# Key chunks of a values tile 400 bytes apart instead of 388, in an attention kernel on one core

## Chip, cores, metric

The kernel runs on one core of one Trainium2 chip. The metric is device time in microseconds (us) of one run; the timed runs of one kernel beside each other lay within about 0.1% here. PE is TensorE (matmul), PEld its weight loads, DVE is VectorE, ACT is ScalarE.

## The reference, cut to what matters

The input `x` (2048 x 640) is normalised; a gated feed-forward branch makes a gate from it, and an attention branch with 32 heads of width 192 makes the value that is gated. Only the last 512 rows of the key and value caches are used.

```python
q = (xn @ wq)                                   # 32 heads x 192
scores = einsum("bhqd,bhkd->bhqk", q, k) * (192 ** -0.5)
p = softmax(scores, axis=-1)                    # over 512 keys
o = einsum("bhqk,bhkd->bhqd", p, v)             # <- the matmuls of this study
s = o.reshape(...) @ wo
return x + s * silu(glu_branch(xn))
```

## The kernel before

The 512 keys are 4 chunks of 128 (`KC = 4`), `DH = 192`. Each of four values tiles holds, in every partition, 4 chunks of 192 values of bf16 (384 bytes) with a column of ones behind each, which makes the softmax denominator come out of the same matmul as a 193rd column, and one column of padding: 194 columns, 388 bytes from chunk to chunk.

```python
    NV = 2 * G                                             # 4 tiles
    v_tiles = []
    for i in range(NV):
        vt = v_pool.tile([P, KC, DH + 2], BF16, name=f"v_sb{i}")
        nc.vector.memset(vt[:, :, DH:DH + 1], 1.0)
        v_tiles.append(vt)
    # ... cut ...
    def load_v(hp, eng):
        # ... cut: tile (2 * hp + i) % NV for head i of pair hp ...
            eng.dma_start(
                vt[:, :, 0:DH],
                A_v_cache[0, hk, Sk - W:Sk, :].rearrange("(p j) d -> p j d", j=KC),
            )
    # ... cut ...
    def stage_pv(n, pp, i):
        # ... cut ...
        E, vt = E_t[n, pp], v_t[hp][i]
        o_ps = bank2()[:, :, 0:2 * OW].rearrange("p b (i n) -> p b i n", i=2)
        for q in range(TQ):                                # 4 blocks of 128 queries
            for c in range(KC):                            # 4 key chunks
                nc.tensor.matmul(                          # L429
                    o_ps[:, q // 2, q % 2, 0:DH + 1], lhsT=E[:, c, i, q * P:(q + 1) * P],
                    rhs=vt[:, c, 0:DH + 1],
                    start=(c == 0), stop=(c == KC - 1),
                )
        # ... cut: reciprocal of column DH, multiply, transpose by DMA ...
```

So a values chunk is the moving operand of a 128x193 matmul, 2048 of them in the program, in groups of 16, and successive matmuls walk the chunks 0, 1, 2, 3, 0, 1, ... of one tile. L397 makes q, L413 the scores, L429 is the value matmul, L474 the output projection.

The softmax here doesn't subtract the row's maximum and nothing guards it: scores larger than these inputs give would overflow.

Of the kernel before, what the change touches and what calls it, by code (L numbers as in the profile page):

```python
# [10 lines left out]
BF16 = mybir.dt.bfloat16  # L11
# [4 lines left out]
def kernel(  # L16
# [14 lines left out]
    P = 128  # L31
# [5 lines left out]
    _, Hkv, Sk, DH = A_k_cache.shape  # L37
# [7 lines left out]
    KC = W // P  # L45
# [50 lines left out]
    v_pool = ctx.enter_context(tc.tile_pool(name="v_pool", bufs=1, **rs))  # L96
# [8 lines left out]
    NV = 2 * G  # L105
    v_tiles = []
    for i in range(NV):
        vt = v_pool.tile([P, KC, DH + 2], BF16, name=f"v_sb{i}")
        nc.vector.memset(vt[:, :, DH:DH + 1], 1.0)
        v_tiles.append(vt)  # L110

# [488 lines left out]
```

## Time and profile before

| | before |
|---|---|
| time, median of the first 3 runs | 932.78 us (932.74 to 933.32) |
| span in the profile | 931.2 us |
| PE busy | 918.3 us, 99% |
| value matmuls (L429): busy, mean duration | 193.7 us, 247 ns |
| PE waiting for others, in all | 3.5 us |

The page of the kernel before, the summary by engine and, in 40 slices of the span, the PE row and the clock row (a 9 is 90% or more):

```profile
PE 918.3 (99%) x7946; PEld 549.5 (59%) x8025; DVE 450.7 (48%) x639; ACT 302.2 (32%) x340; POOL 129.5 (14%) x170
...
PE   9999999999999999999999999999999999999997
...
PEclk9999999999999999999999999999999999999999
```

The waits of PE (engine, tile, line that waited, who was waited for: us in total, times, longest):

```profile
PE ps_all L249 <- DVE warm L244: 1.3, 1, 1.3
PE ps_all L413 <- DVE o_st L436: 1.1, 3, 0.6
PE ps_all L261 <- ACT xnT L276: 0.8, 2, 0.5
PE ps_all L397 <- DVE o_st L436: 0.3, 1, 0.3
```

PE is busy for 99% of the span and waits for almost nothing (3.5 us), at a granted clock of 1.000. But matmuls overlap in this record: each of them lasts 247 ns and the next starts 82 to 87 ns after it, long before it ends. The groups of instructions (busy us, mean ns | idle before), the value line's own view (duration minimum/median/maximum), and the timeline of the first stretch in which value matmuls run alone (start us, length us, group, count):

```profile
L429 PE MATMUL ps_all<-v_sb,E 128*128 128x193 bf16 x2048 | 193.7, 247 | 0.1
```

```profile
L429 PE MATMUL ps_all<-v_sb,E x2048: 243/247/258, 200.8 to 914.5; 128*128 128x193 bf16 x187
```

```profile
200.82 11.05 PE L429 MATMUL ps_all<-v_sb,E 128*128 128x193 bf16 x128
212.47 0.82 PE L413 MATMUL ps_all<-qT,kT 64*128 64x512 bf16 x6 [0.59 <-DVE o_st L436]
```

The last fence: 128 matmuls back to back in 11.05 us. The finest reading is the interval from one matmul's start stamp to the next one's. No view of the profile prints it; it is worked out from the start stamps in the trace and averaged by chunk within the groups of 16 (the first and last matmul of each group left out of the averages by chunk). For the kernel before it is 82.5, 86.3, 85.7, 85.9 ns after chunks 0, 1, 2, 3. (Without the second matmul of each group, whose interval is 87.4 ns, chunk 1 has 86.0 ns, the figure of the prediction.) The sum over four matmuls is taken as a third of the time from the second to the fourteenth start of a group: 340.5 ns, the same in all four tiles.

### The profile page before, as it was taken

The numbers are of one execution on the slowest core, as the hardware profiler recorded it, in microseconds if no ns is written. First come the engines' busy times: TensorE is split into PE (matmuls) and PEld (weight loads), VectorE is DVE, ScalarE is ACT, GpSimd is POOL, SyncE is SP. The second block draws the span as 40 slices with busy tenths as digits, with TensorE's granted clock in tenths as the row PEclk, the third lists the DMA queues.
The fourth block names the chain that finished last, engine by engine and source line by source line (L and its number), as shares of the span: only waits on it lengthen the run. The fifth ranks groups of instructions, "written<-read, shape, count | busy, mean of one in ns | idle before, by whom it ended". The sixth has DMA issues, their size and how long they took to land. (4 is left out here: it accounts for less than half of the span.)

```text
span 931.2 us, 18098 instructions
## 1 busy us (share of the span) xinstructions
PE 918.3 (99%) x7946; PEld 549.5 (59%) x8025; DVE 450.7 (48%) x639; ACT 302.2 (32%) x340; POOL 129.5 (14%) x170
## 2 busy tenths in 40 slices
PE   9999999999999999999999999999999999999997
PEld 5545445465756565656565656566665656566665
DVE  5443532443535454545454444444454545454477
ACT  4333322345141414242423233232323242424320
POOL 0021100010002000200020002000200010395800
PEclk9999999999999999999999999999999999999999
DMA  9544430145425343533453344434342434373755
GB/s 292 146 91 102 67 98 16 57 66 86 80 53 112 77 77 61 111 77 71 67 107 81 57 80 87 102 51 86 77 111 52 86 77 111 75 175 78 148 147 148
DMA packets 176959, 87.17 MB, mean 94 GB/s; under 512 B 152240, under 2 KB 171312, under 8 KB 176880
## 3 DMA queue, kind: packets, MB, share of 16 engines
q1 hardware_dynamic: 146864, 47.20, 26.0%
q0 software_dynamic: 6656, 22.81, 10.1%
q10 hardware_dynamic: 23360, 15.99, 6.2%
q8 instruction: 63, 1.03, 0.5%
q14 instruction: 16, 0.13, 0.1%
HBM read 44.70 MB, written 5.24 MB: 54 GB/s over the span
## 5 line engine op out<-in xcount | busy, mean ns | idle before, releaser
L417 ACT ACTIVATE E<-ps_all 128x1024 bf16<-128x1024 f32 x256 | 246.1, 1023 | 490.4 <-PE ps_all L413 374.2
L402 DVE CAST qT<-ps_all 128x1024 bf16<-128x1024 f32 x96 | 117.5, 1225 | 235.9 <-PE ps_all L397 233.4
L474 PE MATMUL ps_all<-wo_g,oT 128*128 128x128 bf16 (+2 forms) x1474 | 224.3, 295 | 3.2
L397 PE MATMUL ps_all<-xnT,wqp 64*128 64x512 bf16 x960 | 222.2, 376 | 0.3 <-DVE o_st L436 0.3
L397 PE MATMUL ps_all<-xnS,wqp 64*128 64x512 bf16 x960 | 221.4, 376 | 0.0
L429 PE MATMUL ps_all<-v_sb,E 128*128 128x193 bf16 x2048 | 193.7, 247 | 0.1
L413 PE MATMUL ps_all<-qT,kT 64*128 64x512 bf16 x1536 | 184.1, 376 | 1.1 <-DVE o_st L436 1.1
L429 PEld LDWEIGHTS <-E 128*128 128x128 bf16 x2048 | 171.6, 98 | 19.3 <-issue 7.2
L474 PEld LDWEIGHTS <-oT 128*128 128x128 bf16 x1536 | 121.3, 97 | 76.6
L397 PEld LDWEIGHTS <-wqp 64*128 64x128 bf16 x1920 | 100.4, 100 | 107.7 <-issue 0.8
L413 PEld LDWEIGHTS <-kT 64*128 64x128 bf16 x1536 | 74.6, 94 | 91.4 <-issue 6.1
L436 DVE TENSOR_TENSOR o_st<-ps_all,rden 128x768 bf16<-128x768 f32 x128 | 122.6, 957 | 8.1 <-DMA oT<-o_st 3.4
L507 DVE TENSOR_TENSOR acc<-ps_all,acc 128x640 f32<-128x640 f32 x96 | 79.2, 825 | 42.7 <-PE ps_all L474 42.7
L435 DVE RECIPROCAL rden<-ps_all 128x4 f32<-128x4 f32 x128 | 23.3, 182 | 84.4 <-PE ps_all L429 84.2
L131 POOL COPY k_sb<-kn_sb 128x768 bf16<-128x768 bf16 x32 | 25.9, 832 | 274.3 <-DMA kT<-k_sb 227.3
L326 DVE TENSOR_TENSOR hT_sb<-ps_all,sig_sb 128x512 bf16<-128x512 f32 x48 | 33.1, 692 | 51.0 <-PE ps_all L320 41.2
L152 POOL DMA_DIRECT2D wqp<-in_A_wq_dram x16 | 11.8, 741 | 320.9 <-PE ps_all L397 271.8
L320 PE MATMUL ps_all<-xnT,wu_sb 128*128 128x512 bf16 x220 | 55.6, 379 | 0.3
L320 PE MATMUL ps_all<-xnT,wg_sb 128*128 128x512 bf16 x220 | 55.5, 379 | 0.3
L340 PE MATMUL ps_all<-wd_sb,hT_sb 128*128 128x128 bf16 (+1 forms) x377 | 52.4, 298 | 0.4
L325 ACT ACTIVATE sig_sb<-ps_all 128x512 bf16<-128x512 f32 x48 | 28.6, 597 | 56.6 <-PE ps_all L320 56.2
L340 PEld LDWEIGHTS <-hT_sb 128*128 128x128 bf16 x384 | 29.7, 98 | 23.1
(49 smaller groups left out, 271.3 us busy)
## 6 DMA issues: line engine op xcount, KB each, us to landing
wqp<-in_A_wq_dram POOLq DMA_DIRECT2D x16, 480.0 KB, 6.6
wo_g<-in_A_wo_dram ACTq DMA_DIRECT2D x8, 960.0 KB, 5.9
kn_sb<-in_A_k_cache_dram POOLq DMA_DIRECT2D x32, 192.0 KB, 4.5
v_sb<-in_A_v_cache_dram ACTq DMA_DIRECT2D x28, 192.0 KB, 2.9
gB_d<-gB_sb POOLq DMA_DIRECT2D x16, 160.0 KB, 2.2
xnS<-xnT SPq DMA_DIRECT2D x8, 320.0 KB, 4.9
gBa_sb<-gB_d POOLq DMA_DIRECT2D x16, 160.0 KB, 2.9
xa_sb<-in_A_x_dram POOLq DMA_DIRECT2D x16, 160.0 KB, 3.2
```

The source lines that it names most:

```text
L320: nc.tensor.matmul(gu[:, i, :], lhsT=w[:, c, f * P:(f + 1) * P], rhs=xnT[s][:, c, :], start=(c == 0), stop=(c == NCD - 1),)
L325: nc.scalar.activation(sig_sb[:], gu[:, 0, :], AF.Sigmoid)
L326: nc.vector.tensor_tensor(hT_sb[:, f, :], gu[:, 1, :], sig_sb[:], ALU.mult)
L340: nc.tensor.matmul(oB_ps[:, d0:d0 + dsz], lhsT=hT_sb[:, f, q * P:(q + 1) * P], rhs=wd_sb[:, f, d0:d0 + dsz], start=(f == 0), stop=(f == NF ...
L397: nc.tensor.matmul(ps[:, b, :], lhsT=wq_t[g][r, 2 * c + h, u::PC], rhs=x[s][r, c, :], start=(c == 0 and h == 0), stop=(c == NCD - 1 and h ...
L402: nc.vector.tensor_copy(qT_t[n][:, u, :, :], ps)
L413: nc.tensor.matmul(ps[:, b, :], lhsT=kT[r, c * PC + j, :], rhs=qT[r, j, pp, :], start=(j == 0), stop=(j == PC - 1),)
L417: nc.scalar.activation(E_t[n, pp][:, c, :, :], ps, AF.Exp, scale=scale_qk)
L429: nc.tensor.matmul(o_ps[:, q // 2, q % 2, 0:DH + 1], lhsT=E[:, c, i, q * P:(q + 1) * P], rhs=vt[:, c, 0:DH + 1], start=(c == 0), stop=(c = ...
L436: nc.vector.tensor_tensor(o_st[:, :, i * DH:(i + 1) * DH].rearrange("p (b i) d -> p b i d", b=2), o_ps[:, :, :, 0:DH], rden[:].to_broadcas ...
L474: nc.tensor.matmul(oA[:, d0 - base:d0 - base + dsz], lhsT=oT_t[n, pp][:, q * PC + j, :], rhs=wo_t[g][:, cc, d0:d0 + dsz], start=(cc == 0), ...
L507: nc.vector.tensor_tensor(acc[t][:], oA[:, 0:D], acc[t][:], ALU.add)
```

## The change

The intent: make every chunk start on a 16-byte boundary (400 = 25 x 16; 388 is 24 x 16 + 4). The tile bases are multiples of 32 bytes in both built programs. Instructions and their order stay the same on every engine.

```diff
-        vt = v_pool.tile([P, KC, DH + 2], BF16, name=f"v_sb{i}")
+        vt = v_pool.tile([P, KC, DH + 8], BF16, name=f"v_sb{i}")
```

## The prediction

> **What bounds the kernel now.** TensorE. The busy summary gives PE 918.3 us of a 931.2 us span (99%), DVE 48%, ACT 32%; the clock is 9 tenths or more throughout. The waits view charges the matmuls only 3.5 us of waiting. Busy time of pipelined matmuls can flatter, so I read start-to-start times in the trace: each shape keeps its own pitch almost without gaps (512 columns 215-216 ns, 128 columns 55-56 ns). What shortens a matmul's pitch should shorten the span one for one.
>
> **What the change touches.** The 2048 value matmuls (128x193 bf16; values tile moving, E stationary), about 174 us of starts. Every group of 16 walks 4 queries x 4 key chunks. Chunk c starts at base + 388c bytes before, base + 400c after. In the built programs all four bases are multiples of 32 bytes, so before only chunk 0 is 16-byte aligned; chunks 1-3 sit 4, 8 and 12 bytes past such a boundary. No instruction is added or removed, and the order on every engine stays.
>
> The trace separates the chunks. From a chunk's start to the next matmul's:
> - chunk 0: 82.5 ns (duration 244)
> - chunks 1, 2, 3: 86.0, 85.6, 85.9 ns (duration 247)
>
> The view of this line shows the same as minimum 243 and median 247. [...]the others are about 3.3 ns above. Chunk 0 is also the first of each sum, but the 128-column output-projection matmuls keep 55-56 ns whether first or not. [...]3.3 ns is about 8 columns, 16 bytes of bf16, so an estimate: a misaligned start costs one more line. Counting lines doesn't give it: 386 bytes touch 25 lines at offsets 0, 4, 8 and 12 alike.
>
> **Cost.** Removed: (3.5 + 3.1 + 3.4) ns x 512 = 5.1 us, all on PE, all critical. Added: nothing on engines. Moved: each values tile grows by 48 bytes a partition; the value loads still write 384-byte pieces, land in about 3 us, and PE doesn't wait for them. Weight loads take 98 ns but overlap: chunk 0 already runs at 82.5 ns with the same kind of load. DVE and ACT have slack for a 4% faster value stage.
>
> **Predicted time: 927.8 us**, 8 in 10 between 926.7 and 930.0. Chances: faster by over 2% 0.01, within 2% 0.98, slower by over 2% 0.01.
>
> **What would show each step right.** Value matmuls: all four chunks near 82.5 ns start to start, mean duration about 244 instead of 247, busy about 188 us instead of 193.7; other pitches, clock and PE's waits unchanged; span about 5 us shorter.
>
> **What would make it wrong.** (1) The boundary that matters is 32 bytes, not 16: chunks 1 and 3 then sit 16 bytes past one, only chunk 2 gains, about 1.6 us (931.2 us). The trace of before has no moving operand at such an address. (2) Chunk 0 is fast for its place in the sum in this loop alone: no gain. (3) Weight loads back up once all four run at 82.5 ns: part of the gain. (4) The faster value stage makes PE wait for a PSUM bank that DVE empties or for E: the waits view would grow by what is lost.

"The others" are chunks 1 to 3, with 85.8 ns on average about 3.3 ns above chunk 0's 82.5. Intervals of 55 to 56 ns at 128 columns (L261) and 215 to 216 ns at 512 (L320) make about 0.42 ns a column, so 3.3 ns is about 8 columns. That a misaligned start costs one more line was the estimate from these numbers; no trace had shown that lines of 16 bytes exist. That all four chunks would reach 82.5 ns rested on chunk 0 alone.

## The result, and the profile after

| | before | after |
|---|---|---|
| time, median of 4 runs each | 932.91 us | 929.75 us (929.51 to 930.44) |
| ratio, after over before | | 0.9965, 95% interval 0.995 to 0.9979 |
| span in the profile | 931.2 us | 928.1 us |
| value matmuls: start to start, in all | 175.3 us | 171.9 us |
| sum over four value matmuls, as above | 340.5 ns | 333.3 ns |
| intervals after chunks 0, 1, 2, 3 | 82.5, 86.3, 85.7, 85.9 ns | 83.3, 83.3, 83.3, 83.3 ns |

Ratios are those of the record, from fast runs of both kernels in the same rounds; they need not equal the ratio of the medians quoted. The gain is small, but it is clear: in all timed executions the kernel before took 932.56 us or more, and no version with the gain took more than 930.74 us. The same views of the kernel after, first the page (summary, PE and clock rows):

```profile
PE 914.6 (99%) x7946; PEld 546.1 (59%) x8025; DVE 450.7 (49%) x639; ACT 302.1 (33%) x340; POOL 129.5 (14%) x170
...
PE   8999999999999999999999999999999999999997
...
PEclk9999999999999999999999999999999999999999
```

The waits of PE:

```profile
PE ps_all L413 <- DVE o_st L436: 1.4, 3, 0.9
PE ps_all L249 <- DVE warm L244: 1.3, 1, 1.3
PE ps_all L261 <- ACT xnT L276: 1.0, 2, 0.7
PE ps_all L397 <- DVE o_st L436: 0.3, 1, 0.3
PE ps_all L261 <- DMA wu_sb<-in_B_w_up_dram: 0.2, 1, 0.2
```

The group, the line's own view, and the first stretch of value matmuls in the timeline:

```profile
L429 PE MATMUL ps_all<-v_sb,E 128*128 128x193 bf16 x2048 | 190.3, 247 | 0.1
```

```profile
L429 PE MATMUL ps_all<-v_sb,E x2048: 244/247/258, 200.8 to 911.4; 128*128 128x193 bf16 x187
```

```profile
200.84 10.84 PE L429 MATMUL ps_all<-v_sb,E 128*128 128x193 bf16 x128
212.56 0.80 PE L413 MATMUL ps_all<-qT,kT 64*128 64x512 bf16 x5 [0.88 <-DVE o_st L436]
```

PE busy falls by 3.7 us, the value group by 3.4 us, the span by 3.1 us: the gain is all in L429 and lands nearly whole. The first stretch shortens from 11.05 to 10.84 us, but the next score matmul then waits 0.88 instead of 0.59 us for DVE, which gives back 0.3 us once in this execution (in after_again below, the same kernel, that wait was 0.71 us). Two things in these lines don't fit the prediction: the mean duration stayed at 247 ns, and the intervals did not settle at chunk 0's 82.5 ns but at 83.3 ns. Chunk 0 itself became slower. That is what the experiments had to explain.

### The profile page after: what moved, and what is told of

The parts are those of the page before. It is cut to its first block, busy times and chain, and to the rows that moved or that the text cites. A ratio compares the mean times of both kernels' runs of the same rounds, so it can differ in the third digit from the quotient of the medians.

```text
span 928.1 us, 18098 instructions
## 1 busy us (share of the span) xinstructions
PE 914.6 (99%) x7946; PEld 546.1 (59%) x8025; DVE 450.7 (49%) x639; ACT 302.1 (33%) x340; POOL 129.5 (14%) x170
## 5 line engine op out<-in xcount | busy, mean ns | idle before, releaser
L429 PE MATMUL ps_all<-v_sb,E 128*128 128x193 bf16 x2048 | 190.3, 247 | 0.1
L429 PEld LDWEIGHTS <-E 128*128 128x128 bf16 x2048 | 168.5, 98 | 19.3 <-issue 7.2
L507 DVE TENSOR_TENSOR acc<-ps_all,acc 128x640 f32<-128x640 f32 x96 | 79.2, 825 | 42.7 <-PE ps_all L474 42.7
L320 PE MATMUL ps_all<-xnT,wu_sb 128*128 128x512 bf16 x220 | 55.6, 379 | 0.3
L320 PE MATMUL ps_all<-xnT,wg_sb 128*128 128x512 bf16 x220 | 55.5, 379 | 0.3
```

The source lines that it names most:

```text
L320: nc.tensor.matmul(gu[:, i, :], lhsT=w[:, c, f * P:(f + 1) * P], rhs=xnT[s][:, c, :], start=(c == 0), stop=(c == NCD - 1),)
L429: nc.tensor.matmul(o_ps[:, q // 2, q % 2, 0:DH + 1], lhsT=E[:, c, i, q * P:(q + 1) * P], rhs=vt[:, c, 0:DH + 1], start=(c == 0), stop=(c = ...
L507: nc.vector.tensor_tensor(acc[t][:], oA[:, 0:D], acc[t][:], ALU.add)
```

## The experiments

Eleven kernels ran. In what follows "place" is a chunk's address modulo 16 bytes. Edits are against the kernel before. Four runs were timed, in 5 rounds, and all their profiled runs were in the fast state; the others were single looks, of unknown state, and only their intervals in the trace are used (granted clock 0.998 or more in each).

Theory A was the prediction's: a start off a 16-byte boundary costs. Rivals: B, the tile's size and address; C, a change of place between successive matmuls.

### after_again: the change itself, beside the next three

> The changed kernel once more, on one chip with the next runs. About 929.7 us; ratio to before about 0.9966. Value matmuls start to start: 83.3 ns on all four chunks, as in the first trace of it.

Measured: 930.25 us against 933.22 us, ratio 0.9970 (0.9957 to 0.9982); 333.3 ns for four matmuls. The single intervals were 82.9, 83.6, 83.5, 83.4 ns, not all 83.3 as in the first trace. So intervals jitter by some tenths of a ns from execution to execution while their sum does not: the sum is the reading to trust.

### pad_only: the size without the distance

```diff
-        vt = v_pool.tile([P, KC, DH + 2], BF16, name=f"v_sb{i}")
+        vt = v_pool.tile([P, 800], BF16, name=f"v_sb{i}")[:, 0:KC * 194].rearrange("p (c n) -> p c n", c=KC)
```

> The tiles keep the changed kernel's size and base addresses (1600 bytes a tile), but the chunks lie 388 bytes apart as before. Theory A (the cost sits on each value matmul whose moving chunk starts off a 16-byte boundary): the time of before, 932.9 us, ratio 1.000, and the pitches of before by chunk (82.5, 86.0, 85.6, 85.9 ns). Rival B (the gain comes from the tiles' size or where they and their neighbours lie): the time of the changed kernel, 929.7 us, ratio 0.9966.

Measured: 933.35 us, ratio 1.0002 (0.9988 to 1.0015); 340.5 to 340.8 ns by tile. Rival B falls: with the tiles of the changed kernel at its addresses, the distance of 388 bytes still has the full cost. The first stretch in its timeline is as long as before:

```profile
201.20 11.05 PE L429 MATMUL ps_all<-v_sb,E 128*128 128x193 bf16 x128
```

### all_off4: every chunk off the boundary, alike

```diff
-        vt = v_pool.tile([P, KC, DH + 2], BF16, name=f"v_sb{i}")
+        vt = v_pool.tile([P, 808], BF16, name=f"v_sb{i}")[:, 2:2 + KC * 200].rearrange("p (c n) -> p c n", c=KC)
```

> Chunks 400 bytes apart, but each tile starts 4 bytes past a 32-byte boundary, so that all four chunks sit at 4 modulo 16. Theory A: every value matmul pays, also chunk 0. The four pitches of before sum to 340.1 ns; less one aligned pitch of 83.3 ns that leaves 256.8, or 85.6 ns for each misaligned one; so 2048 x (85.6 - 83.3) = 4.7 us over the changed kernel: about 934.4 us, ratio 1.0015 to before, and 85.6 ns on all four chunks. Rival C (the cost comes when successive chunks stand at different places within 16 bytes, as they do at 388): all chunks stand alike, so 83.3 ns and 929.7 us, ratio 0.9966.

Measured: 930.27 us, ratio 0.9970 (0.9957 to 0.9982), the changed kernel's to the digit; 333.3 ns for four matmuls in all tiles. The first stretch of value matmuls in its timeline:

```profile
201.25 10.84 PE L429 MATMUL ps_all<-v_sb,E 128*128 128x193 bf16 x128
```

Theory A, the reason of the prediction, falls: not one of the 2048 chunks starts on a 16-byte boundary, and the whole gain is there.

### offsets: places 0, 4, 8 and 12, one for each tile

```diff
-        vt = v_pool.tile([P, KC, DH + 2], BF16, name=f"v_sb{i}")
+        vt = v_pool.tile([P, 808], BF16, name=f"v_sb{i}")[:, [0, 2, 4, 6][i]:[0, 2, 4, 6][i] + KC * 200].rearrange("p (c n) -> p c n", c=KC)
```

> Chunks 400 bytes apart; the four tiles start 0, 4, 8 and 12 bytes past a 32-byte boundary, so each group of 16 value matmuls has one place within 16 bytes throughout. Theory A: groups of tile 0 at 83.3 ns start to start, the three others at about 85.6 ns (a flat step), or rising with the offset if the cost grows with it. Rival C: 83.3 ns in all four. Time by A: 929.7 + 1536 x 2.3 ns = 933.2 us.

Measured: 333.2, 333.2, 333.3 and 333.3 ns in the four tiles. Alignment is worth nothing at any of these places, as long as the chunks are 400 bytes apart.

So C was left, but another reading fitted as well. A chunk's 193 columns are 386 bytes. At 388 bytes, chunk 0 occupies bytes 0 to 385 and ends in the 16-byte line 384 to 399 (a line here is 16 bytes of addresses from a multiple of 16; that this size matters is for the runs to show); chunk 1 starts at 388, in that very line. The same holds from 1 to 2 and from 2 to 3, but not from 3 back to 0. At 400 bytes no chunk starts in the line in which the one before ended, whatever the base. This is theory D: a matmul whose moving operand starts in the 16-byte line where that of the matmul before it ended pays.

### strides: 388, 392, 396 and 400 bytes in the four tiles

```diff
-        vt = v_pool.tile([P, KC, DH + 2], BF16, name=f"v_sb{i}")
+        vt = v_pool.tile([P, 800], BF16, name=f"v_sb{i}")[:, 0:KC * [194, 196, 198, 200][i]].rearrange("p (c n) -> p c n", c=KC)
```

> The four tiles have chunks 388, 392, 396 and 400 bytes apart (places within 16 bytes 0-4-8-12, 0-8-0-8, 0-12-8-4, 0-0-0-0). Theory A (a misaligned start costs) has fallen. Theory C (a change of place within 16 bytes from one matmul to the next costs) expects all of the first three tiles to pay at each of 4 changes: sums of four pitches about 340.5, 340, 340 and 333.3 ns. Theory D (it costs when a matmul starts in the 16-byte line in which the matmul before it ended: 386 bytes of chunk c and the start of chunk c+1) expects 3, 2, 1 and 0 such events in four matmuls: 340.5, 338.1, 335.7 and 333.3 ns.

Measured: 340.6, 337.7, 335.0 and 333.3 ns, which is D's staircase within 0.7 ns and not C's. The first stretch of value matmuls, which holds all four tiles, lies between 11.05 and 10.84 us:

```profile
201.00 10.94 PE L429 MATMUL ps_all<-v_sb,E 128*128 128x193 bf16 x128
```

The intervals fit D event by event. At 392 bytes they are 82.5, 86.7, 82.5, 85.9 ns: slow after chunks 1 and 3, which start in a line just left (chunk 0 ends at 385 and chunk 1 starts at 392, both in 384 to 399; chunk 2 ends at 1169 and chunk 3 starts at 1176, both in 1168 to 1183), and fast after chunk 2, which starts at 784 while chunk 1 ended at 777, in the line before. Both of those lie in one 32-byte block and are only 6 bytes apart, as the slow pairs are, and the sum, 4.4 ns above 333.3, has room for two events and not for three. So it is the line of 16 bytes that matters, not the closeness; nor is it a line of 8 bytes, since bytes 385 and 392 lie in different blocks of 8 and that pair is slow.

### strides2: the same places, farther apart

```diff
-        vt = v_pool.tile([P, KC, DH + 2], BF16, name=f"v_sb{i}")
+        vt = v_pool.tile([P, 832], BF16, name=f"v_sb{i}")[:, 0:KC * [202, 204, 206, 208][i]].rearrange("p (c n) -> p c n", c=KC)
```

> Chunks 404, 408, 412 and 416 bytes apart: the same places within 16 bytes as 388, 392, 396 and 400, but no chunk starts in the line where the one before ended. Theory C: about 340.5, 340, 340 and 333.3 ns for four matmuls. Theory D: 333.3 ns in all four tiles.

Measured, at 404, 408, 412 and 416 bytes: 333.3, 333.4, 334.2 and 333.3 ns. C falls: 404 bytes repeats the places 0-4-8-12 of the kernel before and costs nothing in the sum. The first stretch of value matmuls:

```profile
201.27 10.85 PE L429 MATMUL ps_all<-v_sb,E 128*128 128x193 bf16 x128
```

The 0.9 ns at 412 bytes is not D's, and is taken up again below. Single intervals need care here. With no shared line they are still uneven: 83.6, 85.0, 82.5, 82.2 ns at 404 bytes and 82.8, 85.7, 82.5, 82.4 ns at 408, where at 416 (places all 0) they are 83.0 to 83.6 ns. The long one follows chunk 1, and shorter ones make up for it. So a slow interval alone is no sign of a shared line; only the sum over four tells what is lost.

### order: 388 bytes, the chunks in another order

```diff
-            for c in range(KC):
+            for k, c in enumerate(((0, 1, 2, 3), (0, 2, 1, 3), (3, 2, 1, 0), (1, 2, 3, 0))[2 * pp + i]):
...
-                    start=(c == 0), stop=(c == KC - 1),
+                    start=(k == 0), stop=(k == KC - 1),
```

The tile was also written as `[P, 776]` and viewed as 4 x 194, which leaves size and addresses as before.

> 388 bytes as before, but the chunks are taken in the order 0-1-2-3, 0-2-1-3, 3-2-1-0 and 1-2-3-0 in the four tiles. Theory C (each step changes the place within 16 bytes in all four orders): about 340 ns for four matmuls in all. Theory D: a shared line only where c+1 follows c: 340.5 ns in the first and the fourth, 333.3 ns in the second and third; in the fourth the fast one of the four pitches moves from the place of chunk 0 to that of the matmul whose neighbours are not adjacent.

Measured: 340.6, 333.5, 335.0 and 340.8 ns. The first, second and fourth are D's. The first stretch of value matmuls, all four orders together:

```profile
201.30 10.96 PE L429 MATMUL ps_all<-v_sb,E 128*128 128x193 bf16 x128
```

In the fourth the fast interval (82.2 ns) follows chunk 0 although that now comes last in the sum, so being first in the sum was never the reason. The third, 3-2-1-0, is 1.7 ns above what D expects: a miss, see strides3.

### columns: what an undisturbed matmul costs

```diff
-        E, vt = E_t[n, pp], v_t[hp][i]
+        E, vt, n_v = E_t[n, pp], v_t[hp][i], ((193, 194, 195, 196), (197, 198, 199, 200), (192, 191, 190, 189), (188, 186, 184, 180))[2 * pp + i]
...
-                    o_ps[:, q // 2, q % 2, 0:DH + 1], lhsT=E[:, c, i, q * P:(q + 1) * P],
-                    rhs=vt[:, c, 0:DH + 1],
+                    o_ps[:, q // 2, q % 2, 0:n_v[q]], lhsT=E[:, c, i, q * P:(q + 1) * P],
+                    rhs=vt[:, c, 0:n_v[q]],
```

The chunks were 400 bytes apart with ones from column 192 on, and the reciprocal read column 179, since the shorter matmuls don't write column 192 (wrong result).

> Aligned chunks 400 bytes apart, and from 180 to 200 columns a matmul (wrong result on purpose: fewer than 193 columns leave out the denominators). It asks what the 83.3 ns of an undisturbed value matmul is made of[...]. If a matmul costs its columns plus a fixed part: 0.42 ns more per column, 78 ns at 180, 82.9 at 192, 86.3 at 200. If whole 16-byte lines of the moving row count (8 columns): 80 ns up to 192 columns and 83.3 ns for all from 193 to 200. If weight loads hold the stream: 83.3 ns also below 193 columns.

(The 0.42 ns a column is an estimate that the trace of the kernel before gives, (215.5 - 55.5) ns / 384 columns; the times for 180, 192 and 200 columns follow, to 0.1 ns or so, from it and from the 83.3 ns measured at 193.)

Measured, mean interval by number of columns:

| columns | 180 | 184 | 188 | 189 | 190 | 191 | 192 | 193 | 194 | 195 | 196 | 199 | 200 |
|---|---|---|---|---|---|---|---|---|---|---|---|---|---|
| ns | 77.6 | 79.2 | 80.9 | 81.8 | 81.8 | 82.6 | 82.5 | 83.3 | 83.5 | 84.2 | 84.2 | 85.9 | 85.9 |

(186, 197 and 198 columns gave 80.1, 85.0 and 85.1 ns.) This is columns plus a fixed part, with an odd number counted as the next even one within 0.2 ns (193 and 194 columns: 83.3 and 83.5 ns; 199 and 200: 85.9 ns both): the table rises by 8.3 ns over 20 columns, about 0.42 ns a column, which leaves an estimate of 2 to 3 ns as the fixed part. Whole lines of 8 columns don't show, and weight loads (98 ns each, overlapped) don't hold the stream at 83.3 ns, as 180 columns run at 77.6 ns. So 83.3 ns is the mean interval of an undisturbed stream of 193-column matmuls, and the 82.5 ns after chunk 0 in the kernel before, which equals the interval of 192 columns, was not a rate that any run's stream of 193-column matmuls kept.

### order_0213: the gain without touching the layout

```diff
-            for c in range(KC):
+            for k, c in enumerate((0, 2, 1, 3)):
...
-                    start=(c == 0), stop=(c == KC - 1),
+                    start=(k == 0), stop=(k == KC - 1),
```

> The kernel before, 388 bytes apart, with one edit: the chunks are taken in the order 0-2-1-3, so that no matmul starts in the 16-byte line in which the one before it ended. Theory D: the whole gain without touching the layout: 333.4 ns for four value matmuls instead of 340.5, ratio to before 0.997 (about 930 us), as the changed kernel has. Theory A (alignment of the start) and theory C (change of place): three of four chunks are still off a 16-byte boundary and the place changes at each step, so no gain, ratio 1.000.

Measured: 930.17 us against 933.19 us, ratio 0.9969 (0.9955 to 0.9983); 333.3 to 333.5 ns for four. With 388 bytes, all but chunk 0 misaligned, and not a byte moved, the kernel has the changed kernel's time. (Its single intervals are 82.5, 85.8, 82.5 and 82.6 ns: one is still as slow as in the kernel before, and the sum is not.) The first stretch in its timeline is the changed kernel's too:

```profile
201.14 10.84 PE L429 MATMUL ps_all<-v_sb,E 128*128 128x193 bf16 x128
```

It does not beat the change: 930.17 us and, in after_again, 930.25 us are the same. Both reach the sum of an undisturbed stream, and no run shows a faster stream of 193 columns.

### shared: aligned and shared, misaligned and not shared

```diff
-        vt = v_pool.tile([P, KC, DH + 2], BF16, name=f"v_sb{i}")
-        nc.vector.memset(vt[:, :, DH:DH + 1], 1.0)
+        vt = v_pool.tile([P, 784], BF16, name=f"v_sb{i}")
+        nc.vector.memset(vt[:], 1.0)
...
+        E, vt, (w, n_v) = E_t[n, pp], v_t[hp][i], ((192, 193), (194, 186), (192, 192), (193, 193))[2 * pp + i]
...
-                    rhs=vt[:, c, 0:DH + 1],
+                    rhs=vt[:, c * w:c * w + n_v],
```

The output slice is `0:n_v`, the load of a tile writes chunks `w` columns apart, and the reciprocal reads column 179 as above.

> Wrong result on purpose. Tile 0: chunks 384 bytes apart (all starts aligned to 16), 193 columns, so that the last column read is the first of the next chunk's line: theory D expects three shared lines in four matmuls, about 340.5 ns although every start is aligned; theory A 333.3. Tile 1: 388 bytes apart (misaligned as before), 186 columns, no shared line: theory D expects the plain 186-column time, 4 x 80.07 = 320.3 ns; theory A about 7 more, 327. Tile 2: 384 bytes apart, 192 columns, neighbours without a gap but no shared line: theory D 4 x 82.5 = 330 ns. Tile 3: 386 bytes apart, 193 columns, packed without a gap, three shared lines: theory D about 340.5 ns.

Measured: 340.6, 320.1, 330.0 and 341.1 ns, all within 0.6 ns of D. The first tile is the sharpest single test: every chunk starts on a 16-byte boundary, and four matmuls cost exactly what they cost in the kernel before, because the 193rd column lies in the line where the next chunk begins. The second is its mirror: misaligned at 388 bytes, but seven columns shorter, it runs at the undisturbed rate of 186 columns. In the third the chunks follow each other without a gap but share no line, and it runs at the rate of 192 columns (4 x 82.5 ns): closeness by itself costs nothing.

### strides3: is the small rest real?

```diff
-        vt = v_pool.tile([P, KC, DH + 2], BF16, name=f"v_sb{i}")
+        vt = v_pool.tile([P, 4 * [210, 206, 214, 202][i]], BF16, name=f"v_sb{i}")[:, 0:KC * [210, 206, 214, 202][i]].rearrange("p (c n) -> p c n", c=KC)
```

> Chunks 420, 412, 428 and 404 bytes apart, no shared lines. Theory D alone expects 333.3 ns for four matmuls in all. The run of strides2 had 334.2 at 412 bytes (places 0-12-8-4), 0.8 above, which D doesn't explain. If that comes with the step from place 0 to place 12, then 412 and 428 bytes show about 334.2 again and 420 and 404 (0-4-8-12) show 333.3; if it was chance, all show 333.3.

Measured, at 420, 412, 428 and 404 bytes: 333.3, 334.3, 334.2 and 333.3 ns. The rest is real: about 0.9 ns in four matmuls where the places run 0-12-8-4, none where they run 0-4-8-12. In the order 3-2-1-0 the places run 12-8-4-0, the same cycle, and the rest was 1.7 ns. In 412, 428 and 3-2-1-0 the slow interval (86.7 to 87.0 ns) follows the chunk at place 12 that comes after one at place 0. Whether it is that step that costs, or the falling order of the places, and why once 0.9 and once 1.7, is open. It also means that the 1.7 ns at 396 bytes, which has one shared line and the same step at the same matmul, can't be split between the two. The kernels before and after don't contain the step.

## Why the prediction was right or wrong

The time and its direction were right; the reason given was not, and the size rested on one misread number. In part that is luck. The trace of the kernel before tied the cost to chunks 1 to 3, and padding to 400 bytes takes it away whether the cause is alignment or a shared line, so a wrong reason gave the right direction. The forecast gain was 5.1 us and the measured one 3.2 us: 929.75 us lies 0.25 us inside the upper end of the stated range, and in after_again the same kernel took 930.25 us.

- **What bounds the kernel: right.** The stream of matmuls on PE sets the time. The value matmuls' starts took 3.4 us less in all and the span 3.1 us less; PE's waits went from 3.5 to 4.2 us, 0.4 us of that at L261, before the attention.
- **"A misaligned start costs one more line": wrong.** All_off4 has no aligned chunk and the full gain (333.3 ns for four); the first tile of shared has only aligned chunks and the full cost (340.6 ns). What costs in these runs is a start in the 16-byte line where the matmul before ended. In the kernel before that befell chunks 1, 2 and 3, the very ones that are misaligned, so its trace could not tell the two apart. The prediction had noticed that 386 bytes touch 25 lines at every place, which should have counted against its reason: it looked at lines within a matmul, and the cost sits between two of them. The change works because 400 bytes moves each start out of the line before, not because it aligns it.
- **"(3.5 + 3.1 + 3.4) ns x 512 = 5.1 us": mis-sized.** This is the term that failed in the sum. It took the interval after chunk 0, 82.5 ns, for the rate that all four would reach. The rate of undisturbed 193-column matmuls is 83.3 ns, so four cost 333.3 and not 330 ns. The saving is 340.5 - 333.3 = 7.2 ns, times 512 is 3.7 us; 0.3 us of it went into the one longer wait for DVE after the first stretch, which leaves the 3.4 us of the starts in this pair of profiles. A slow and a fast interval next to each other should have been summed before one of them was taken for a price.
- **Mean duration 247 to 244, busy to 188 us: wrong.** Duration stayed at 247 and busy fell to 190.3 us. Order_0213 has the same time with a mean of 246. Durations followed neither theory.
- **What the change adds and moves, weight loads, other pitches: right.** Loads of values landed in 3.1 us instead of 2.9 (median), and PE waited for none. Weight loads did not hold the stream (98 ns each, and 180 columns ran at 77.6 ns). Other intervals stayed, 55 to 56 ns at L261 (128 columns) and 215 to 216 ns at L320 (512 columns) in both traces.
- **What would make it wrong:** the boundary of 32 bytes (1) was not it, as chunks 1 and 3 of the changed kernel, 16 bytes past one, run at 83.3 ns like the others; place in the sum (2) was excluded by the order run; weight loads (3) by the columns run; a wait for DVE (4) appeared, with 0.3 us.

Shown is where the cost arises (line, order, number) and its size, 2.2 to 2.4 ns for each shared line from the tiles of 392 and 388 bytes (2.6 ns at 386). Every shared line in these runs came from bf16 matmuls of 193 columns, an odd number; whether an even number pays the same was not tried. What in the hardware produces the cost is not shown by any run.

## What to carry to other kernels

When matmuls run back to back and their moving operands lie one behind the other, check in which 16-byte line each ends and the next begins: padding the row, or walking the chunks in another order, removed 2.2 to 2.4 ns for each coincidence here, where the matmuls had 193 columns. That was 2% of the value matmuls' time (340.5 to 333.3 ns) and 0.3 to 0.35% of the kernel, where PE was busy for 99% of the span. Other shapes were not tried. And a correlation in one trace ("the aligned chunk is the fast one") is a suspicion: shift everything alike before calling it the cause.
